# Bucketed attention and a maxout FFN: heads 4 to 7 of the first batch prepared as one set of four

## The chip, the cores and the metric

The kernel runs on one core of one Trainium2 chip. The metric is the device time of one execution in microseconds (us); lower is better. A core has five engines that run side by side, each through its own queue in order: TensorE (PE, with its weight loads PEld), VectorE (DVE), ScalarE (ACT), GpSimd (POOL) and SyncE (SP), which here only issues DMAs. POOL and ACT issue DMAs too.

## The reference: what is computed

Shapes: `q`, `k`, `v` are (4 batches, 8 heads, 768 tokens, 64), `proj` is (64, 6), the three input weights are (512, 768) and the output weight is (768, 512).

```python
def _attn_ref(q, k, v, proj):
    scale = 1.0 / np.sqrt(D)
    q_bits = (np.einsum('bhsd,dk->bhsk', q, proj) > 0)
    k_bits = (np.einsum('bhsd,dk->bhsk', k, proj) > 0)
    powers = 2 ** np.arange(n_bits)
    q_bucket = np.sum(q_bits * powers, axis=-1)
    k_bucket = np.sum(k_bits * powers, axis=-1)
    mask = q_bucket[:, :, :, None] == k_bucket[:, :, None, :]
    scores = scale * np.matmul(q, k.transpose(0, 1, 3, 2))
    scores = np.where(mask, scores, -1000000000.0)
    scores = scores - np.max(scores, axis=-1, keepdims=True)
    attn = np.exp(scores)
    attn = attn / (np.sum(attn, axis=-1, keepdims=True) + 1e-09)
    return np.matmul(attn, v)

def _moe_ref(x, w1, w2, w3, w_out):
    h = np.maximum(np.maximum(x @ w1, x @ w2), x @ w3)
    return h @ w_out
```

Each query attends only to the keys whose six hash bits equal its own. The attention's output, heads side by side, is the FFN's input.

## The kernel before

**How the mask enters.** For every head there is a tile S of 64 + 6 (later batches 64 + 8) rows by 768 tokens in bf16: the 64 scaled values of a token in a column, and under them its hash bits as +0.5 or -0.5. One matmul of a key tile's S with a query tile's S gives score plus a bonus for equal bits; the exponential's bias takes the bonus off again, so that tokens with a differing bit fall to nothing. What this study is about is how S is made.

**Units.** `units` cuts the attention into 192 units, 48 for each batch. A unit is one head, one chunk of queries (256 wide in batch 0, 384 later) and some key blocks: `scores(u)` (lines 277 to 301) puts 2 or 3 matmuls of S (L293) into one of two score buffers, and ACT takes the exponential of the buffer (L301). In batch 0 units 0 to 23 are heads 0 to 3 and units 24 to 47 heads 4 to 7, in the order head 4, 5, 6, 7 of chunk 0 first. So the S of head 4 is read first by unit 24.

**The order of work** is written out by hand. The last loop goes over u: at u it issues `scores(u + 1)`, then whatever `when(u, ...)` has put there, then FFN pieces by a credit, then the attention sums (L345) and values (L367) that `todo` has for u. Each engine executes its share in just that order. Sums and values of heads 0 to 3 stand at u = 20 to 30. A `hash_at` entry at u runs `quad_hash` at the end of u and puts the sending of its bits at u + 1. Later `when` entries for the same u stand behind earlier ones.

**Heads pair by pair (batch 0).** `load_pair` brings two heads of q and k into a tile `nat`, tokens in the partitions. `pair_group` turns three 128 x 128 blocks on PE against an identity (L120) and lets DVE copy the result from PSUM into `t32` (L129; for pair 1 in part ACT, L127). `pair_place` scales and narrows it to bf16 on POOL straight into S (L134). The bits of pairs 0 and 1 are computed head by head (`head_rest`, L167 on PE, L172 on DVE straight into S); pairs 2 and 3, heads 4 to 7, have `pair_hash`: four matmuls for a pair (L147), one DVE comparison into a tile `bits` (L150), and four DMAs from SP into S (L156). In `pair_hash` the transposed data are in fp32, as in all hashing.

**Heads in sets of four (batches 1 to 3).** A set is four heads of one side, q or k: set (1, g) is k, set (0, g) is q. `load_quad` brings each head with a DMA of its own into 32 partitions of `nat`. `turn` is one DVE transpose of 32 x 32 blocks (L198); a set needs four, u = 0, 1 for the half of the features and half = 0, 1. `narrow` scales a half of the features to bf16 on POOL (L203). The heads now lie under each other in partitions, so `place` moves each of the four with a DMA from SP into its S (L208). `quad_hash` computes all bits of q and k of four heads with eight matmuls (L217) and one comparison (L220); four more SP DMAs send them into S (L228).

**Queues that matter here.** SP carries, in this order: the first loads, the sends of bits of pairs 2 and 3, the loads of set 3 (u = 23 and 27), places and bits of set 2, and so on. POOL carries L134 and L203 and also issues the DMAs for V, the FFN weights and most `nat` loads: those of (1, 2) at u = 1 and (0, 2) at u = 13, V at u = 17, weights at u = 3, 12, 21, 31. A DMA issue waits until the one issued eight places earlier on the same kind of queue has landed.

Of the kernel before, what the change touches and what calls it, by code (L numbers as in the profile page):

```python
# [11 lines left out]
BF16 = mybir.dt.bfloat16  # L12
AluOp = mybir.AluOpType
# [4 lines left out]
def kernel(  # L18
# [12 lines left out]
    nc = tc.nc  # L31
    B, H, S, D = q.shape
    NBITS = proj.shape[1]
    P = 128
    NM = S // P
    HALF = S // 2
    MH = NM // 2
# [3 lines left out]
    Q = 32  # L41
    CC = P // Q
# [19 lines left out]
    b_pool = ctx.enter_context(tc.tile_pool(name="bpool", bufs=2))  # L62
# [13 lines left out]
    pj2 = konst.tile([P, Q], FP32, name="pj2")  # L76
# [11 lines left out]
    def bank():  # L88
        i = free_banks.pop(0)
        return i, bank_tiles[i]  # L90

    def give(i):
        free_banks.append(i)


    nat, t32, t16, s_of, where, v_at = {}, {}, {}, {}, {}, {}

    def start_set(name, heads):
        nat[name] = nat_pool.tile([P, 4 * NM * D], FP32, tag="nat", name="nat")
        for x, key in enumerate(heads):  # L100
            where[key] = (name, x)
# [7 lines left out]
    def load_pair(pi, eng, sides=(1, 0), h0=0, h1=2):  # L109
        if pi not in nat:  # L110
            start_set(pi, [(0, 2 * pi), (0, 2 * pi + 1), (1, 2 * pi), (1, 2 * pi + 1)])
        n = nat[pi].rearrange("p (s h w) -> p s h w", s=2, h=2)
        for side in sides:
            src = (q, k)[side][0, 2 * pi + h0 : 2 * pi + h1].rearrange("h (p c) d -> p h (c d)", p=P)
            eng.dma_start(n[:, side, h0:h1, :], src)
# [23 lines left out]
        pair_keep(pi, side, hd, mp, eng)  # L139
        give(i)  # L140

    def pair_hash(pi):
        i, bp = bank()
        for side in (1, 0):
            for hd in range(2):
                g = 2 * side + hd
                nc.tensor.matmul(bp[Q * g : Q * (g + 1), 0:HALF], pj2[:, :],  # L147
                                 t32[pi][:, side, hd * HALF : (hd + 1) * HALF], start=True, stop=True)
        bits = b_pool.tile([P, HALF], BF16, tag="bits", name="bits")
        nc.vector.tensor_scalar(out=bits[:], in0=bp[:, 0:HALF], scalar1=0.0, scalar2=0.5,  # L150
                                op0=AluOp.is_gt, op1=AluOp.subtract)
        give(i)
        for hd in range(2):
            for side in (1, 0):
                g = 2 * side + hd
                nc.sync.dma_start(s_of[pi][D : D + NBITS, g, :].rearrange("b (c n) -> b c n", c=2),  # L156
                                  bits[Q * g : Q * g + 2 * NBITS, :])


    def first_place(side, hd, par, mp):  # L160
        nc.scalar.mul(s_tile(0)[0:D, 2 * side + hd, par * HALF : (par + 1) * HALF],
                      mp[par * D : (par + 1) * D, 0:HALF], RS)
# [22 lines left out]
    def load_quad(side, g, xs, eng):  # L185
        if (side, g) not in nat:
            start_set((side, g), [(side, 4 * g + x) for x in range(4)])
        for x in xs:
            b, h = divmod(4 * g + x, H)
            src = (q, k)[side][b, h].rearrange("(cc t m) d -> t cc (m d)", cc=CC, t=Q)  # L190
            dst = nat[side, g][x * Q : (x + 1) * Q, :].rearrange("t (cc w) -> t cc w", cc=CC)
            eng.dma_start(dst, src)  # L192

    def turn(name, u, half):
        if name not in t32:
            t32[name] = t32_pool.tile([P, 2, S], FP32, tag="T32", name="T32")
        i_ = nat[name].rearrange("p (cc m u d) -> p u m cc d", cc=CC, u=2, d=Q)[:, u, half * MH : (half + 1) * MH]
        nc.vector.transpose(t32[name][:, u, half * HALF : (half + 1) * HALF], i_)  # L198

    def narrow(name, u):  # L200
# [244 lines left out]
    def when(u, f, *args):  # L445
        at.setdefault(u, []).append(lambda: f(*args))

    with tc.manual_schedule():
# [5 lines left out]
        load_pair(0, nc.sync, (1,), 1, 2)  # L454
        load_pair(0, nc.scalar, (0,), 1, 2)
        load_pair(1, nc.sync)
        load_pair(2, nc.sync)
        load_pair(3, nc.sync)
        nc.gpsimd.memset(pj[:], 0.0)
        nc.vector.memset(pj2[:], 0.0)  # L460
        nc.vector.memset(ones[:], 1.0)
# [44 lines left out]
            for par in range(2):  # L506
                pair_place(0, side, par, 1, 2)

        for pi, us in ((1, ((0, 1, 0), (0, 0, 0), (3, 1, 1), (4, 0, 1))), (2, ((6, 1, 0), (7, 1, 1), (8, 0, 0), (9, 0, 1))),
                       (3, ((13, 1, 0), (14, 1, 1), (15, 0, 0), (16, 0, 1)))):  # L510
            for u, side, hd in us:
                when(u, pair_group, pi, side, hd, nc.scalar if pi == 1 and hd == 1 else None)
                if pi == 1:
                    for par in range(2):
                        when(u, pair_place, pi, side, par, hd, hd + 1)
                elif hd == 1:
                    for par in range(2):
                        when(u, pair_place, pi, side, par)
        when(2, head_rest, 0, 1)
        when(2, t32.pop, 0)  # L520
        when(5, head_rest, 1, 0)
        when(10, pair_hash, 2)
        when(11, t32.pop, 2)
        when(11, head_rest, 1, 1)
        when(12, t32.pop, 1)
        when(17, pair_hash, 3)
        when(18, t32.pop, 3)
        when(1, load_quad, 1, 2, range(4), nc.gpsimd)
        when(17, load_v, 1)
        for n, u in ((0, 3), (1, 12), (2, 21), (3, 31)):  # L530
# [1 line left out]
        when(13, load_quad, 0, 2, range(4), nc.gpsimd)  # L532
        for u, side, g in ((23, 1, 3), (27, 0, 3)):
            when(u, load_quad, side, g, range(4), nc.sync)
        hash_at = {}
        for g in range(2, NQUAD):
            b2, i2 = divmod(g, 2)
            need = UPB * b2 + 12 * i2
            for n, side in enumerate((1, 0)):
                name = (side, g)  # L540
                if g > 3:
                    for x in range(4):
                        when(need - 36 + 4 * n + x, load_quad, side, g, (x,), nc.gpsimd)
                t0 = need - {2: 26, 3: 23}.get(g, 21) + 4 * n
                for n2 in range(4):
                    when(t0 + n2, turn, name, n2 // 2, n2 % 2)
                for u2 in range(2):
                    when(t0 + 2 + 2 * u2, narrow, name, u2)
                when(t0 + 6, place, name, range(4))
            hash_at[{2: 33, 3: 47}.get(g, need - 11)] = g  # L550
            when({2: 36, 3: 46}.get(g, need - 22), load_v, g)
# [4 lines left out]
        for c, i in sorted(done_at, key=lambda e: done_at[e]):  # L556
            d = done_at[c, i] + (LAG if c < 3 else 2)
            sums, values = burst(c, i)
            pieces = [lambda f=sums: f(0, NM), lambda f=values: f(0, 0, NM), lambda f=values: f(1, 0, NM)]
            for n, f in enumerate(pieces):  # L560
                u = {(0, 0): (20, 21, 22), (1, 0): (24, 25, 26), (2, 0): (28, 29, 30)}.get((c, i), (d, d, d))[n]
# [64 lines left out]
```

## Time and profile before

| | |
|---|---|
| time, median of 3 runs | 277.81 us (276.68 to 278.61) |
| the profiled execution's own time | 277.43 us |
| its span, first to last instruction | 275.6 us |
| mean granted TensorE clock | 0.992 |
| S of heads 4 to 7, pair by pair: PE turns L120, of 48 in all | 24 |
| one copy L129 on DVE | 0.49 us |
| one place L134, 64 x 768, on POOL | 0.83 us |
| one transpose L198 on DVE | 0.57 us, four end to end about 0.5 each |
| one narrow L203 on POOL, 128 x 768 | 0.82 us |
| one DMA issue L192 on POOL | 0.55 us |

The page gives first the busy time of each engine, then the span in 40 slices, the DMA queues, the chain of work that ended last, and the costliest groups of instructions. A timeline row reads: start in us from the span's start, duration, engine, line, operation, tiles, number of instructions merged, and in brackets how long the engine was idle before it and what ended that. SPq and POOLq are issues of DMAs by these engines' sequencers. PE's records are modelled at their ends and overlap a little. The trace also has the moments at which a DMA's completion signals arrive; where a landing time is given, it is the last of these for that DMA.

### The profile page before, as it was taken

Reading aid. Unit: us, or ns where it says so; the run is one execution under the profiler, and the core shown is the slowest. Engines: PE = TensorE matmul, PEld = TensorE weight load, DVE = VectorE, ACT = ScalarE, POOL = GpSimd, SP = SyncE. Lnnn points to the kernel's source line nnn. Section 1 sums busy time; section 2 is a strip of 40 time slices with the busy share of each in tenths; the row PEclk is TensorE's granted clock in tenths of the full one; section 3 lists DMA queues with packets and bytes.
Section 4 is the critical chain, followed back from the end, with each engine's and each line's share of the span. In section 5 each row is a group of like instructions: output and inputs, shape, how many; then the busy total and the mean of one; then the engine's idle time right before and its main releaser. Section 6 shows DMA issues by size and latency. Waiting matters only on the chain.

```text
span 275.6 us, 6502 instructions
## 1 busy us (share of the span) xinstructions
PE 263.2 (95%) x2538; PEld 158.6 (58%) x2538; DVE 196.0 (71%) x486; ACT 179.1 (65%) x260; POOL 68.0 (25%) x108
## 2 busy tenths in 40 slices
PE   7899999999999979999999999999999999999992
PEld 3555667865666645565555555555555555555651
DVE  3686787965886996996684898797657674865440
ACT  2888876648767860966859586683868769571321
POOL 3699550374100350285000062140000000000000
PEclk9999999999999997999999999999999999999999
DMA  7979999979921157169912036622020003001203
GB/s 226 287 158 165 221 245 227 209 125 231 246 49 40 38 145 115 53 183 251 168 40 76 2 81 148 160 57 63 33 95 0 1 4 114 2 0 40 76 2 114
DMA packets 20398, 30.97 MB, mean 112 GB/s; under 512 B 2608, under 2 KB 14736, under 8 KB 20368
## 3 DMA queue, kind: packets, MB, share of 16 engines
q0 software_dynamic: 8384, 14.16, 26.9%
q1 hardware_dynamic: 11552, 15.88, 19.2%
q10 hardware_dynamic: 432, 0.52, 0.6%
q8 instruction: 20, 0.33, 0.5%
q14 instruction: 10, 0.08, 0.1%
HBM read 25.17 MB, written 6.29 MB: 114 GB/s over the span
## 4 chain that ended last, share of the span: by engine, by line
PE 86%; DVE 7%; ACT 2%; issue 2%; DMA 1%; DVEq 0%; ACTq 0%
PE ms L396 31%; PE sc L293 22%; PE ms L367 11%; PE ms L433 11%; PE ms L345 4%; PE ms L217 3%; ACT AT L301 2%; DVE ad L324 2%; PE ms L472 1%; DVE ht L405 1%; PE ms L120 1%; PE ms L147 1%; PE ms L167 1%; DVE S L172 1%; DMA out_dram<-osb 1%
## 5 line engine op out<-in xcount | busy, mean ns | idle before, releaser
L301 ACT ACTIVATE AT<-sc 128x768 f16<-128x768 f32 x192 | 152.7, 816 | 66.4 <-PE sc L293 58.6
L396 PE MATMUL ms<-xT,w_sb 128*128 128x384 f16 (+1 forms) x648 | 115.0, 308 | 0.7 <-DVE ht L405 0.7
L293 PE MATMUL sc<-S 72*128 72x384 bf16 (+1 forms) x432 | 93.5, 308 | 2.6 <-ACT AT L301 1.9
L396 PEld LDWEIGHTS <-w_sb 128*128 128x128 f16 x648 | 62.6, 97 | 36.9 <-issue 1.5
L405 DVE TENSOR_TENSOR ht<-ht,ms 128x384 f16<-128x384 f16 (+1 forms) x108 | 54.3, 503 | 37.3 <-PE ms L396 35.4
L293 PEld LDWEIGHTS <-S 72*128 72x128 bf16 (+1 forms) x432 | 39.5, 98 | 34.0 <-issue 14.1
L203 POOL TENSOR_SCALAR T<-T 128x768 bf16<-128x768 f32 x24 | 21.8, 907 | 101.2 <-DVE T L198 80.4
L367 PE MATMUL ms<-AT,vo 128*32 128x385 f16 (+3 forms) x864 | 37.7, 318 | 0.0
L433 PE MATMUL ms<-wout_sb,ht 128*128 128x512 f16 x138 | 35.4, 378 | 0.0
L367 PEld LDWEIGHTS <-vo 128*32 128x32 f16 x864 | 25.1, 99 | 9.3 <-issue 1.3
L324 DVE TENSOR_TENSOR ad<-AT,AT 128x768 f16<-128x768 f16 x48 | 27.4, 572 | 2.8 <-ACT AT L301 2.8
L324 DVE TENSOR_TENSOR ad<-ad,AT 128x768 f16<-128x768 f16 x48 | 26.5, 551 | 2.5 <-ACT AT L301 1.2
L198 DVE STREAM_TRANSPOSE T<-nat 128x384 f32<-128x384 f32 x48 | 26.6, 561 | 0.0
L401 ACT CAST ht<-ms 128x384 f16<-128x384 f32 x36 | 17.2, 477 | 8.8 <-PE ms L396 8.7
L374 DVE SCALAR_TENSOR_TENSOR xT<-ms,sv,rb 128x384 f16<-128x384 f32 (+1 forms) x36 | 19.9, 568 | 2.6 <-PE ms L367 1.3
L433 PEld LDWEIGHTS <-ht 128*128 128x128 f16 x138 | 13.3, 97 | 13.3 <-DVE ht L405 0.8
L437 ACT COPY osb<-ms 128x512 f32<-128x512 f32 x23 | 13.4, 582 | 10.7 <-PE ms L433 9.6
L352 DVE STREAM_TRANSPOSE ys<-ms 128x384 f32<-128x384 f32 (+1 forms) x18 | 9.7, 536 | 8.0 <-PE ms L345 7.8
L134 POOL TENSOR_SCALAR S<-T 64x384 bf16<-64x384 f32 (+1 forms) x21 | 13.2, 627 | 3.8 <-ACT T L127 1.6
L192 POOL DMA_DIRECT2D nat<-in_k_dram x20 | 11.1, 563 | 3.6 <-DMA nat<-in_k_dram 2.2
L192 POOL DMA_DIRECT2D nat<-in_q_dram x20 | 11.1, 566 | 2.7 <-DMA vo<-in_v_dram 1.8
L345 PEld LDWEIGHTS <-ones 128*32 128x32 f16 x240 | 5.4, 95 | 8.8 <-issue 8.7
(48 smaller groups left out, 121.9 us busy)
## 6 DMA issues: line engine op xcount, KB each, us to landing
out_dram<-osb SPq DMA_DIRECT2D x23, 256.0 KB
S<-T SPq DMA_DIRECT2D x48, 96.0 KB
nat<-in_k_dram POOLq DMA_DIRECT2D x20, 192.0 KB, 7.5
nat<-in_q_dram POOLq DMA_DIRECT2D x20, 192.0 KB, 7.1
vo<-in_v_dram POOLq DMA_DIRECT2D x8, 384.0 KB, 8.2
w_sb<-in_moe_w_dram POOLq DMA_DIRECT2D x3, 768.0 KB, 7.2
nat<-in_k_dram SPq DMA_DIRECT2D x6, 192.0 KB
nat<-in_k_dram SPq DMA_DIRECT2D x3, 384.0 KB
```

The costliest lines, as they stand in the source:

```text
L192: eng.dma_start(dst, src)
L198: nc.vector.transpose(t32[name][:, u, half * HALF : (half + 1) * HALF], i_)
L203: nc.gpsimd.tensor_scalar(out=t16[name][:, u, :], in0=t32[name][:, u, :], scalar1=RS, scalar2=1.0, op0=AluOp.mult, op1=AluOp.mult)
L293: nc.tensor.matmul(views[j], s_of[kn][0 : D + bits, kx, m * P : (m + 1) * P], s_of[qn][0 : D + bits, qx, q0 : q0 + w], start=True, stop=True)
L301: nc.scalar.activation(t[:, :, 0:w], whole, ActFn.Exp, bias=-SCALE * 0.25 * bits, scale=SCALE)
L324: nc.vector.tensor_tensor(out=sum_of[c, h][:], in0=t[0], in1=t[n], op=AluOp.add)
L367: nc.tensor.matmul(av[Q * x : Q * (x + 1), 0:n], v_at[2 * b + i][:, x, cb * D + side : (cb + 1) * D : 2], weights_of(c, 4 * i + x, m)[:, 0 ...
L374: nc.vector.scalar_tensor_tensor(out=xt_of(c)[:, 2 * i + side, 0:w], in0=av[:, 0:w], scalar=sv_of[b, i, side][:], in1=rb[0][:, 0:w], op0=A ...
L396: nc.tensor.matmul(ps[:, 0:w], w_sb[wi][:, jc, fb * P : (fb + 1) * P], xt[:, jc, 0:w], start=(jc == 0), stop=(jc == NJC - 1))
L401: nc.scalar.copy(hts[fb][:, 0:w], ps[:, 0:w])
L405: nc.vector.tensor_tensor(out=hts[fb][:, 0:w], in0=hts[fb][:, 0:w], in1=ps[:, 0:w], op=AluOp.max)
L433: nc.tensor.matmul(ps[:, 0:DM], hts[fb][:, tb * P : (tb + 1) * P], wout_sb[:, fb, :], start=(fb == 0), stop=(fb == NFB - 1))
```

## The change

Heads 4 to 7 of batch 0 become sets (1, 1) for k and (0, 1) for q. The loads of pairs 2 and 3 (four DMAs of two heads each) become eight DMAs of one head each, k first. The 24 PE turns, eight DVE copies, eight POOL places and two `pair_hash` of these pairs go. In their place come four DVE turns and two POOL narrows for k at u = 6 to 9 and the same for q at u = 10, 12, 13, 14, four place DMAs behind each (u = 9 and u = 14), one `quad_hash` at u = 16, and its four sends at u = 17. `turn` takes every second token block for g = 1, since batch 0 keeps its tokens in the pairs' order (`block_of`). The new `when` entries stand in the program behind those for loads and weights. On POOL the order from u = 7 on is thus: narrow and narrow of k, one weight load (u = 12), first narrow of q (u = 12), the four loads of set (0, 2) (u = 13), second narrow of q (u = 14), then V and weights. On SP it is: eight loads, four places of k, four places of q, four sends of bits, then the loads of set 3.

```diff
-    def pair_hash(pi):
-        i, bp = bank()
-        for side in (1, 0):
-            for hd in range(2):
-                g = 2 * side + hd
-                nc.tensor.matmul(bp[Q * g : Q * (g + 1), 0:HALF], pj2[:, :],
-                                 t32[pi][:, side, hd * HALF : (hd + 1) * HALF], start=True, stop=True)
...
-                nc.sync.dma_start(s_of[pi][D : D + NBITS, g, :].rearrange("b (c n) -> b c n", c=2),
-                                  bits[Q * g : Q * g + 2 * NBITS, :])
...
     def turn(name, u, half):
...
-        i_ = nat[name].rearrange("p (cc m u d) -> p u m cc d", cc=CC, u=2, d=Q)[:, u, half * MH : (half + 1) * MH]
+        ms = slice(half, NM, 2) if name[1] == 1 else slice(half * MH, (half + 1) * MH)
+        i_ = nat[name].rearrange("p (cc m u d) -> p u m cc d", cc=CC, u=2, d=Q)[:, u, ms]
         nc.vector.transpose(t32[name][:, u, half * HALF : (half + 1) * HALF], i_)
...
         load_pair(1, nc.sync)
-        load_pair(2, nc.sync)
-        load_pair(3, nc.sync)
+        for side in (1, 0):
+            load_quad(side, 1, range(4), nc.sync)
...
-        for pi, us in ((1, ((0, 1, 0), (0, 0, 0), (3, 1, 1), (4, 0, 1))), (2, ((6, 1, 0), (7, 1, 1), (8, 0, 0), (9, 0, 1))),
-                       (3, ((13, 1, 0), (14, 1, 1), (15, 0, 0), (16, 0, 1)))):
+        for pi, us in ((1, ((0, 1, 0), (0, 0, 0), (3, 1, 1), (4, 0, 1))),):
...
-                elif hd == 1:
-                    for par in range(2):
-                        when(u, pair_place, pi, side, par)
...
-        when(10, pair_hash, 2)
-        when(11, t32.pop, 2)
         when(11, head_rest, 1, 1)
         when(12, t32.pop, 1)
-        when(17, pair_hash, 3)
-        when(18, t32.pop, 3)
         when(1, load_quad, 1, 2, range(4), nc.gpsimd)
...
-        hash_at = {}
+        for side, us in ((1, (6, 7, 8, 9)), (0, (10, 12, 13, 14))):
+            for n, u in enumerate(us):
+                when(u, turn, (side, 1), n // 2, n % 2)
+                if n % 2:
+                    when(u, narrow, (side, 1), n // 2)
+            when(us[3], place, (side, 1), range(4))
+        hash_at = {16: 1}
```

More of the change, by code (lines that the diff above doesn't have):

```diff
@@ L140, in pair_group @@
         give(i)
-    def pair_hash(pi):
-        i, bp = bank()
-        for side in (1, 0):
-            for hd in range(2):
-                g = 2 * side + hd
-                nc.tensor.matmul(bp[Q * g : Q * (g + 1), 0:HALF], pj2[:, :],
-                                 t32[pi][:, side, hd * HALF : (hd + 1) * HALF], start=True, stop=True)
[L149 to L155, printed above, removed]
-                nc.sync.dma_start(s_of[pi][D : D + NBITS, g, :].rearrange("b (c n) -> b c n", c=2),
-                                  bits[Q * g : Q * g + 2 * NBITS, :])
     def first_place(side, hd, par, mp):
```

## The prediction

> **What bounds the kernel now.** I read the page's busy shares and its chain first, for the engine that sets the end, and then the timelines of ACT, PE, POOL and SP around the changed units, for what that stretch waits on.
>
> ```profile
> PE 263.2 (95%) x2538; PEld 158.6 (58%) x2538; DVE 196.0 (71%) x486; ACT 179.1 (65%) x260; POOL 68.0 (25%) x108
> ...
> PE 86%; DVE 7%; ACT 2%; issue 2%; DMA 1%; DVEq 0%; ACTq 0%
> ```
>
> TensorE sets the end over the whole span. But the page's share is an average, and the changed work lies in units 6 to 17. ACT's timeline there:
>
> ```profile
> 14.87 4.37 ACT L301 ACTIVATE AT<-sc 128x768 f16<-128x768 f32 x6
> 20.61 0.81 ACT L301 ACTIVATE AT<-sc 128x768 f16<-128x768 f32 x1 [1.37 <-PE sc L293]
> 21.80 4.40 ACT L301 ACTIVATE AT<-sc 128x768 f16<-128x768 f32 x6 [0.39 <-PE sc L293]
> 27.00 2.21 ACT L301 ACTIVATE AT<-sc 128x768 f16<-128x768 f32 x3 [0.80 <-PE sc L293]
> ```
>
> These are units 6 to 11, 12, 13 to 18, and 19 to 21. Inside a run one exponential follows the other every 0.72 us (4.37 less the last one's 0.81, over 5): here ACT is the bound, and PE has room. ACT waits only at the three hashes: 1.37 behind the first `pair_hash`, 0.39 behind `head_rest`, 0.80 behind the second. PE's timeline shows where that ends:
>
> ```profile
> 27.86 0.49 PE L293 MATMUL sc<-S 70*128 70x256 bf16 x3 [0.57 <-ACT AT L301]
> 28.28 0.84 PE L345 MATMUL ms<-AT,ones 128*32 128x256 f16 x24
> 29.05 0.50 PE L293 MATMUL sc<-S 70*128 70x256 bf16 x3
> 29.49 0.85 PE L367 MATMUL ms<-AT,vo 128*32 128x257 f16 x24
> 30.27 0.50 PE L293 MATMUL sc<-S 70*128 70x256 bf16 x3
> 30.70 0.85 PE L367 MATMUL ms<-AT,vo 128*32 128x257 f16 x24
> ```
>
> Unit 21's scores (27.86) are the last that wait for ACT; from then on PE is full to the end but for some 3 us. So whatever moves unit 21 moves the end, and any later wait of PE is paid whole. The next L293 row starts at 31.49: unit 24, the first that reads the S of head 4.
>
> **The change, part by part.**
>
> *PE turns, copies, places that go.* The 24 turns are about 2.7 us of PE (groups of three, 0.34 from row to row), but at units 6 to 11 ACT ran without a gap over them: worth nothing. DVE loses eight copies of 0.49 and gains eight transposes of about 0.5: even. POOL loses eight places of 0.83 and gains four narrows of 0.82.
>
> *Hashes.* The two `pair_hash` and their waits of 1.37 and 0.80 go; one `quad_hash` comes (42.70 to 44.13 in set 2: 1.43 of PE). I step the engines with the rows' durations. ACT ends unit 10 at 18.5, so unit 12's scores, `head_rest` and unit 13's scores stand 1.55 earlier than now (18.5 for 20.07), and ACT starts unit 13 at 20.25 and unit 17 at 23.1. DVE: bits of `head_rest(1, 0)` until 17.3, four turns of k until 19.3, one of q until 19.8, then the bits of `head_rest(1, 1)`, 2.26 for four, until 22.1, and the other three turns of q at 22.7, 23.2 and 23.65. The hash stands behind unit 17's scores (22.5). Its second half needs the last turn, so it starts at 23.7 and PE goes on 0.75 later, at 24.45; ACT starts unit 18 at 25.0 (0.54 behind its scores, as now) against 25.4 now, unit 19 at 25.7 against 27.0, and unit 21's scores come at 26.55 against 27.86. **Gain: 1.3.** Unit 24 could start at 31.49 - 1.3 = 30.2.
>
> *The way of S to unit 24.* This is what is late next. POOL does the narrow of q's first half at 22.75 to 23.6 (second turn at 22.7). Behind it stand the four loads of set (0, 2), now at
>
> ```profile
> 23.22 2.23 POOL L192 DMA_DIRECT2D nat<-in_q_dram  x4
> ```
>
> so the second narrow of q runs from about 26.0 to 26.85. SP must hold the four places of q until then, and the sends of bits, though the bits are ready at 25.1, stand behind them in SP's queue. Set 3 shows the same eight issues with nothing to hold them:
>
> ```profile
> 56.65 2.49 SPq L208 DMA_DIRECT2D S<-T  x4
> 59.33 2.94 SPq L228 DMA_DIRECT2D S<-bits  x4
> ```
>
> The third send, q's first half of the tokens, starts 4.2 us behind the first place. Unit 24 waits for it: 26.9 + 4.2 = 31.1. Already the issue is later than 30.2. How long it takes to land is the open price. By the completion signals the sends of the second `pair_hash`, at 27.15 to 29.45 and alone on their queue, landed 5.1 to 6.2 us later, while POOL's weights and loads filled the DMA engines (share over 1 in that stretch). From below: the fastest send of the trace took 2.6 (21.77 to 24.4). From above: in set 3 the third send landed 13.9 behind the first place (56.65 to 70.5), with POOL's loads beside it. Set 2, 44.02 to 54.6, gives 10.6. As landing times that is 33.7, 36.3 (31.1 + 5.2), 37.5 and 40.8. I take 37.0, between the two that are nearest in place and in order. **PE waits from 30.2 to 37.0: 6.8.** Nothing covers it: PE's queue is in order, and sums of the next chunk, values and scores all stand behind unit 24. The places of k are free (narrowed by 20.65, sent by 23), as are the first loads: the eighth issues at about 8.4, and what SP loads now lands by 14.4, before the first turn at 17.3.
>
> *The clock.* What does PE pay after so long a wait? The trace has one such place, in windows of PE busy, PEld, DVE, ACT, POOL, granted clock, DMA share, GB/s:
>
> ```profile
> 102.00:104.00 2.00, 0.38 (x7) 0.13 (x10) 1.90 (x6) 0.21 (x1) 1.28 (x2) 1.00 0.10 14
> 104.00:106.00 2.00, 2.00 (x28) 1.27 (x31) 1.39 (x5) 0.00 (x0) 0.00 (x0) 0.51 0.92 100
> 106.00:108.00 2.00, 2.00 (x36) 1.31 (x29) 1.04 (x2) 0.00 (x0) 0.00 (x0) 0.64 1.19 238
> ```
>
> After two mostly idle microseconds the clock is halved from 104.0 to 107.5, and the chain gives 48 L367 matmuls 3.37 there against 1.97 elsewhere. **1.4 more.** [...]
>
> **Sum.** -1.3 + 6.8 + 1.4 = **+6.9**. The profiled execution took 277.4 (its span of 275.6 and 1.8 around it), 0.4 under the median of the three runs; I predict **284.3 us**.
>
> **The rivals.**
>
> *S lands fast.* SP alone feeds its queue then, and 24 KB is little. At the fastest latency, 2.6, the bits land at 33.7: a wait of 3.5, less 1.3, and too short for a halved clock: +2.2, 279.6. For it: the first sends of the trace. Against it: those had only one weight load beside them; here two more, V and four loads are queued. [...] Chance 0.13.
>
> *S comes in time, and the kernel is faster.* Place: SP's queue. If the second narrow of q and SP's eight issues ran some 7 us earlier than I step them (bits landed by 30.2, the point from which it decides), only the gain of 1.3 would remain: 276.1. For it: set 2's S had 1.5 us to spare at unit 48 (landed by 54.8, read at 56.32). Against it: the order of POOL and SP is fixed, and the transposes stand behind 2.26 us of bits on DVE. Chance 0.05.
>
> *The queue is shared as in set 3.* Landing at 40.8: a wait of 10.6, one or two halved windows: -1.3 + 10.6 + 1.4 to 2.8, +10.7 to +12.1, 288 to 289.5. For it: set 3 has the same eight DMAs in the same order beside POOL loads of the same kind. Against it: there eight such loads were issued right beside the places, here four, already under way. Chance 0.12.
>
> **Chances and range.** My own case has 0.70, with landings from 35.6 to 39.4: 282.9 to 286.7. The range reaches from the fast landing, 279.6, to the foot of the third rival, 288.0. About 1% (2.8 us) is what a measurement can tell from no change: faster by more needs twice the gain I find, 0.02; within it lie the fast landing and the case in time, 0.16; slower 0.82.
>
> **What would show it.** A wait of PE before the second-half scores (unit 24, about 30 to 37), ended by DMAs into S, and ACT idle for about 7 us with it; the ACT gap behind the first `pair_hash` gone, and a gap of about 1.2 at unit 18; unit 21's scores near 26.5; a clock of 0.5 for a few us after the wait; POOL's second narrow of q right behind four L192 issues; SP's places of q from about 27. Wrong would be: scores of unit 24 following at once (then S was in time); PE's row at 26.5 not earlier than now (then DVE's turns hold the hash longer). A step of the clock somewhere else, as at 104, is worth 1.4 by itself.

## The result, and the profile after

| | before | after |
|---|---|---|
| median of four runs each | 277.88 us (276.68 to 278.61) | 290.98 us (287.76 to 291.76) |
| profiled execution, and its span | 277.43, 275.6 | 291.76, 290.0 |
| mean granted TensorE clock | 0.992 | 0.946 |

The ratio is 1.045 (95% interval 1.036 to 1.054): 13.1 us slower. 284.3 had been forecast, with a range up to 288.0. The direction holds, the size is twice what was forecast. Line numbers of the kernel after are lower by 17 or 18: scores L276, exponential L284, sums L328, values L350, `turn` L181, `narrow` L186, `place` L191, `quad_hash` L200, its sends L211.

The page of the kernel after, busy time by engine and two rows of the 40 slices (7.25 us each):

```profile
PE 271.3 (94%) x2514; PEld 158.8 (55%) x2514; DVE 195.8 (68%) x485; ACT 179.3 (62%) x260; POOL 64.9 (22%) x104
...
PE   7989939999999998799999999999999999999993
...
PEclk9985575999999999799999999999999999999999
```

PE is 8.1 us busier with 24 instructions fewer: the same matmuls take longer. The row PEclk says why. Slices 3 to 7 have a clock of 0.5 to 0.8, and before had 0.9 or more in all of them; the 7 further right is the old place at 104, now at 118. The slice with a 3 in PE's row is the forecast wait. So two things are seen, and only one of them had been expected where it starts.

ACT's timeline of the kernel after, units 6 to 12 in the first row:

```profile
15.34 5.15 ACT L284 ACTIVATE AT<-sc 128x768 f16<-128x768 f32 x7
21.78 1.51 ACT L284 ACTIVATE AT<-sc 128x768 f16<-128x768 f32 x2 [1.29 <-PE sc L276]
23.47 1.51 ACT L284 ACTIVATE AT<-sc 128x768 f16<-128x768 f32 x2 [0.18 <-PE sc L276]
25.17 0.81 ACT L284 ACTIVATE AT<-sc 128x768 f16<-128x768 f32 x1 [0.18 <-PE sc L276]
28.64 1.51 ACT L284 ACTIVATE AT<-sc 128x768 f16<-128x768 f32 x2 [2.66 <-PE sc L276]
...
41.98 1.51 ACT L284 ACTIVATE AT<-sc 128x768 f16<-128x768 f32 x2 [5.81 <-PE sc L276]
```

The wait of 1.37 behind the first `pair_hash` is gone as forecast: unit 12's exponential runs on without a gap. But the next waits are longer than those of before (1.29 for 0.39, 2.66 for 0.80). PE's timeline shows what ACT waits for:

```profile
18.35 0.49 PE L276 MATMUL sc<-S 70*128 70x256 bf16 x3 [0.21 <-ACT AT L284]
...
25.06 2.79 PE L200 MATMUL ms<-T,pj 128*32 128x384 f32 x16
27.78 1.46 PE L276 MATMUL sc<-S 70*128 70x256 bf16 x6
...
33.08 1.48 PE L350 MATMUL ms<-AT,vo 128*32 128x257 f16 x24
34.50 0.82 PE L276 MATMUL sc<-S 70*128 70x256 bf16 x3
35.25 1.48 PE L350 MATMUL ms<-AT,vo 128*32 128x257 f16 x24
41.08 1.44 PE L276 MATMUL sc<-S 70*128 70x256 bf16 x6 [4.35 <-issue]
```

A burst of 24 values takes 1.48 where it took 0.85, a score of three matmuls 0.82 for 0.50, the `quad_hash` 2.79 where the same sixteen matmuls take 1.50 later on. Then, at 41.08, comes unit 24 after 4.35 us of nothing. The windows of the kernel after, cut where the clock changes (us, PE busy, PEld, DVE, ACT, POOL, granted clock, DMA share, GB/s):

```profile
12.84:16.26 3.42, 3.02 (x27) 1.60 (x26) 2.96 (x6) 3.34 (x7) 3.26 (x7) 1.00 1.03 231
16.26:19.68 3.42, 2.48 (x19) 1.40 (x23) 3.33 (x7) 3.42 (x6) 3.03 (x7) 1.00 1.00 191
19.68:23.09 3.41, 3.15 (x17) 1.21 (x11) 2.57 (x6) 2.12 (x4) 2.19 (x3) 0.50 0.96 187
...
33.33:36.74 3.41, 3.40 (x51) 1.62 (x43) 1.66 (x5) 1.48 (x2) 0.00 (x0) 0.50 1.22 226
36.74:40.16 3.42, 0.00 (x0) 0.00 (x0) 1.58 (x4) 0.00 (x0) 0.82 (x1) 1.00 1.08 230
40.16:43.57 3.41, 2.49 (x30) 1.49 (x30) 0.00 (x0) 1.51 (x2) 0.00 (x0) 0.50 1.09 238
43.57:46.98 3.41, 3.41 (x46) 1.50 (x42) 2.58 (x7) 0.87 (x2) 0.83 (x1) 0.50 0.95 204
46.98:50.40 3.42, 3.42 (x50) 1.96 (x46) 1.55 (x4) 2.08 (x3) 0.83 (x1) 0.50 0.45 111
```

In before, PE is busy through the same units; its window there, in the same columns:

```profile
16.00:19.40 3.40, 3.40 (x28) 2.30 (x26) 3.19 (x7) 3.24 (x5) 3.08 (x6) 1.00 0.88 174
```

In after, the clock is halved from 19.68, 17 us ahead of the wait, just behind the window in which PE had little but scores to do (19 matmuls, one score every 0.70 us, where ACT is the bound). It stays halved for five windows, is full in the window in which PE does nothing, and is halved for three more windows, to 50.40, after the wait.

POOL's and SP's timelines of the kernel after, where S of heads 4 to 7 is made:

```profile
24.00 0.82 POOL L186 TENSOR_SCALAR T<-T 128x768 bf16<-128x768 f32 x1 [1.99 <-DVE T L181]
24.88 2.25 POOL L174 DMA_DIRECT2D nat<-in_q_dram  x4
27.19 0.83 POOL L186 TENSOR_SCALAR T<-T 128x768 bf16<-128x768 f32 x1
```

```profile
21.21 9.30 SPq L191 DMA_DIRECT2D S<-T  x8
30.61 3.03 SPq L211 DMA_DIRECT2D S<-bits  x4
```

This order is the forecast one, an issue of four loads between the two narrows of q and the bits behind all places, some 1.2 us later than stepped. The third send of bits is issued at 32.27, and by its completion signals it lands at 41.0; PE goes on at 41.08.

Against before, the 14.4 us between the two spans are then: unit 24 could start at 36.7 instead of 31.5, 5.2 later (0.5 of it a later start of the whole kernel); the wait, 4.35; the halved clock behind it, 4.15 more between 41 and 50.4; 0.7 in the rest. The first two are one sum: unit 24 starts 9.6 later, and what it starts on is the landing of S at 41.0, so a PE that came sooner would only wait longer (the first experiment shows it).

### The profile page after: what moved, and what is told of

It reads as the page before. It is cut to its first block, busy times and chain, and to the rows that moved or that the text cites. A ratio compares the mean times of both kernels' runs of the same rounds, so it can differ in the third digit from the quotient of the medians.

```text
span 290.0 us, 6458 instructions
## 1 busy us (share of the span) xinstructions
PE 271.3 (94%) x2514; PEld 158.8 (55%) x2514; DVE 195.8 (68%) x485; ACT 179.3 (62%) x260; POOL 64.9 (22%) x104
## 4 chain that ended last, share of the span: by engine, by line
PE 78%; DVE 8%; ACT 4%; DMA 3%; issue 3%; POOL 1%; SPq 1%; DVEq 0%; ACTq 0%
PE ms L379 28%; PE sc L276 19%; PE ms L350 11%; PE ms L416 10%; PE ms L328 4%; ACT AT L284 3%; PE ms L200 3%; DMA S<-bits 3%; DVE ad L307 2%; DVE S L154 2%; PE ms L455 1%; DVE ht L388 1%; PE ms L149 1%; DVE T L181 1%; SPq L191 1%
## 5 line engine op out<-in xcount | busy, mean ns | idle before, releaser
L284 ACT ACTIVATE AT<-sc 128x768 f16<-128x768 f32 x192 | 152.9, 815 | 80.1 <-PE sc L276 72.2
L276 PE MATMUL sc<-S 72*128 72x384 bf16 (+1 forms) x432 | 98.7, 325 | 8.9 <-issue 4.7
L379 PEld LDWEIGHTS <-w_sb 128*128 128x128 f16 x648 | 62.7, 97 | 36.8 <-issue 1.5
L276 PEld LDWEIGHTS <-S 72*128 72x128 bf16 (+1 forms) x432 | 41.2, 102 | 45.3 <-issue 21.5
L186 POOL TENSOR_SCALAR T<-T 128x768 bf16<-128x768 f32 x28 | 25.1, 897 | 117.4 <-DVE T L181 89.0
L350 PE MATMUL ms<-AT,vo 128*32 128x385 f16 (+3 forms) x864 | 40.2, 334 | 0.0
L350 PEld LDWEIGHTS <-vo 128*32 128x32 f16 x864 | 25.6, 103 | 11.0 <-issue 1.6
L181 DVE STREAM_TRANSPOSE T<-nat 128x384 f32<-128x384 f32 x56 | 30.6, 560 | 0.0
L307 DVE TENSOR_TENSOR ad<-ad,AT 128x768 f16<-128x768 f16 x48 | 26.5, 552 | 2.5 <-ACT AT L284 1.2
L416 PEld LDWEIGHTS <-ht 128*128 128x128 f16 x138 | 13.4, 97 | 13.1 <-DVE ht L388 0.6
L200 PE MATMUL ms<-T,pj 128*32 128x384 f32 x112 | 12.2, 543 | 0.0
L328 PEld LDWEIGHTS <-ones 128*32 128x32 f16 x240 | 5.9, 106 | 9.8 <-issue 9.0
```

What stands on the lines that cost most here:

```text
L186: nc.gpsimd.tensor_scalar(out=t16[name][:, u, :], in0=t32[name][:, u, :], scalar1=RS, scalar2=1.0, op0=AluOp.mult, op1=AluOp.mult)
L200: nc.tensor.matmul(bp[Q * r : Q * (r + 1), 0:HALF], pj[:, u, :], ts[side][:, u, j * HALF : (j + 1) * HALF], start=(u == 0), stop=(u == 1))
L276: nc.tensor.matmul(views[j], s_of[kn][0 : D + bits, kx, m * P : (m + 1) * P], s_of[qn][0 : D + bits, qx, q0 : q0 + w], start=True, stop=True)
L284: nc.scalar.activation(t[:, :, 0:w], whole, ActFn.Exp, bias=-SCALE * 0.25 * bits, scale=SCALE)
L307: nc.vector.tensor_tensor(out=sum_of[c, h][:], in0=t[0], in1=t[n], op=AluOp.add)
L350: nc.tensor.matmul(av[Q * x : Q * (x + 1), 0:n], v_at[2 * b + i][:, x, cb * D + side : (cb + 1) * D : 2], weights_of(c, 4 * i + x, m)[:, 0 ...
```

## The experiments

Theory 1, formed from these views: the whole loss is (a) a clock that falls because the 24 turns of PE are gone from units 6 to 17, and (b) the way of S to unit 24, with the halved clock behind that wait. Its rivals are that the clock falls for another reason than the missing turns, or that the wait alone explains the loss.

**PE kept busy where the turns were.** Three turns of the identity into a PSUM bank of their own, the kind of work that the change removed, at each of units 6 to 19.

```diff
+    def keep_busy():
+        i, mp = bank()
+        for n in range(MH):
+            nc.tensor.transpose(mp[:, n * P : (n + 1) * P], iden[:], iden[:])
+        give(i)
...
+        for u in range(6, 20):
+            when(u, keep_busy)
```

> The changed kernel plus a filler on TensorE: at each of units 6 to 19 three 128x128 fp32 turns of the identity into a spare PSUM bank that nobody reads (42 turns, about 0.36 us a unit, in PE's room beside the exponential's 0.72). Theory 1 (the missing turns let the clock fall at 19.7): granted clock 1.0 up to the wait, unit 24's scores ready at about 31 instead of 36.7; but S still lands at about 40 to 41, since POOL's and SP's order and the load on the DMA engines stay, so the wait grows from 4.4 to 9 or 10 us, the clock falls in it, and the time is 289 to 292, about that of the changed kernel. Theory 2 (the clock's fall at 19.7 has another cause): clock 0.5 from about 20 as in the changed kernel, unit 24 ready at 36 to 38, 290 to 293.

Measured 290.43 us, ratio 1.043 (1.037 to 1.049). PE's timeline of this run:

```profile
26.50 1.50 PE L206 MATMUL ms<-T,pj 128*32 128x384 f32 x16
...
32.87 0.85 PE L356 MATMUL ms<-AT,vo 128*32 128x257 f16 x24
42.24 1.44 PE L282 MATMUL sc<-S 70*128 70x256 bf16 x6 [8.52 <-DMA nat<-in_k_dram]
43.61 1.47 PE L334 MATMUL ms<-AT,ones 128*32 128x256 f16 x24
```

The `quad_hash` is back at 1.50 and the values at 0.85: the clock is 1.0 from 15.2 to 35.68, through the stretch in which it had been halved. So it is the missing work that let the clock fall here. The time hardly changes, 0.5 us and within the noise, since PE arrives 3.0 us earlier (33.72 for 36.73) and waits for S all the longer, 8.52: the third send of bits, issued at 33.66, lands at 42.15, and PE goes on at 42.24. (The releaser named on the row is a load that lands later; by the signals it is the bits.) Behind the wait the clock is again halved until 49.33. So in the changed kernel the clock lost ahead of unit 24 is hidden behind the wait, and what sets the time is the landing of S and the clock after it. The profiled execution also has a halved window ahead of the identity turns, 11.79 to 15.20, behind a wait of 0.58 for the q of pair 1; more on that at the end of this section.

**No wait for S.** The changed kernel, in which the scores of heads 4 to 7 of batch 0 read the S of heads 0 to 3; the S of heads 4 to 7 is still made.

```diff
-        (qn, qx), (kn, kx) = where[0, b * H + h], where[1, b * H + h]
+        hs = b * H + h - (4 if b == 0 and h >= 4 else 0)
+        (qn, qx), (kn, kx) = where[0, hs], where[1, hs]
```

> The changed kernel, but the scores of heads 4 to 7 of batch 0 read the S of heads 0 to 3 (their q, k and bits, so the values of these heads are others); turns, narrows, places and bits of heads 4 to 7 are still done and read by nobody. So the wait for S is gone and all work stays. Theory 1: the clock falls at about 19.7 all the same and is back at about 37; no wait before unit 24, no second fall; 5.2 us (unit 24 at 36.7 for 31.5) over before, 283 to 284. Theory 2 (all the loss hangs on the wait): 276.5 to 278.

Measured 281.56 us, ratio 1.011 (1.005 to 1.017), between the two forecasts. The wait and what it brings behind it are thus worth 9.4 of the 13.1 us. The windows of this run around the fall of the clock, columns as above:

```profile
17.73:21.14 3.41, 2.67 (x23) 1.26 (x22) 3.15 (x7) 3.08 (x5) 3.09 (x6) 1.00 0.96 173
21.14:24.55 3.41, 2.41 (x22) 1.19 (x20) 3.35 (x7) 3.36 (x5) 1.98 (x3) 1.00 1.01 193
24.55:27.96 3.41, 3.15 (x20) 1.12 (x16) 0.56 (x2) 1.32 (x3) 3.22 (x7) 0.50 1.00 175
```

The clock falls here with no wait of PE longer than 0.57 us in the two windows before, behind a window with 2.41 of 3.41 us busy, and stays halved until 34.79: three windows, not five. One of the four runs, 279.01 us at a mean clock of 0.993, loses little.

**Both together.**

> Both: filler on TensorE at units 6 to 19, and heads 4 to 7 of batch 0 read the S of heads 0 to 3 (other values; their own S is made and not read). This leaves only the gain that I had put at 1.3 us. Theory 1: clock 1.0 through units 6 to 30, no wait, 276 to 278 (the filler may cost a few tenths at the hash). If the filler does not hold the clock up: like the run without filler, 283 to 284.

Measured 279.37 us, ratio 1.003 (0.999 to 1.006, ten runs). With the wait gone, the clock ahead of unit 24 is worth another 2.2 us in the medians; the intervals of the two runs overlap, so that this is a rough figure. What remains against before, 1.5 us in the medians (the interval includes no change), misses the 276 to 278 expected, and it is not the gain of 1.3 that I had forecast for the changed kernel without its wait. The profiled execution, at 281.93 us the longest of the ten, shows two losses that Theory 1 leaves out: a wait of 0.68 for the q of pair 1 with a halved window behind it (12.96 to 16.37), and a stop of PE of 1.01 us up to 39.27, in the middle of the values, for which the profile names no releaser.

**The kernel before, without its 24 turns.** The other direction: only the turns of pairs 2 and 3 are left out (DVE still copies the banks, so heads 4 to 7 hold no right data).

```diff
-        pair_turn(pi, side, hd, mp)
+        if pi < 2:
+            pair_turn(pi, side, hd, mp)
```

> The kernel before, with the 24 PE turns of pairs 2 and 3 left out (DVE copies what stands in the bank, so S and bits of heads 4 to 7 hold no meaningful values); all else as before, the two pair hashes too. Theory 1: with PE half idle in units 6 to 9 the clock falls in a window near 16 to 23 and PE becomes the bound there: unit 24 later by 2 to 6 us, 280 to 284. Theory 2: PE had room, so the turns cost nothing and save nothing: 277 to 278, clock 0.99.

Four runs: 283.32, 283.15, 283.32 and 279.0 us, median 283.23. With 2.7 us of PE's work taken away, the kernel is no faster in any of them, and 5.4 us slower in three. (The ratio on record, 1.0105 with an interval of 1.0004 to 1.0207, takes in only two of the runs, 283.15 and 279.0; in the run of 279.0 the mean clock was 0.999, in the other three 0.962 to 0.964.) Its windows, columns as above:

```profile
14.58:17.99 3.41, 2.38 (x18) 1.27 (x17) 3.28 (x7) 3.41 (x6) 3.17 (x6) 1.00 0.95 233
17.99:21.41 3.42, 3.42 (x16) 0.96 (x19) 1.45 (x3) 1.09 (x3) 3.04 (x5) 0.50 0.99 159
21.41:24.82 3.41, 2.41 (x21) 1.20 (x14) 2.58 (x5) 2.91 (x5) 3.41 (x6) 1.00 0.73 109
24.82:28.23 3.41, 3.41 (x16) 1.12 (x16) 1.83 (x5) 2.24 (x3) 2.78 (x4) 0.50 1.08 218
```

Twice a window with 2.4 us of PE, scores and little else, is followed by a halved one. The kernel before has a mean clock of 0.990 to 0.999 in every one of its runs here; the profiled one, with the window at 104 alone, has 0.992, so none of them had room for windows like these. So the turns, which cost nothing on the path, had been holding the clock; one run escaped, and on what that hangs no run shows.

**S sooner, clock kept.** Then the way of S, with the identity turns in place. POOL's four loads of set (0, 2) go two units later; of the places of q only head 4's stay ahead of the bits.

```diff
-        when(13, load_quad, 0, 2, range(4), nc.gpsimd)
+        when(15, load_quad, 0, 2, range(4), nc.gpsimd)
...
-            when(us[3], place, (side, 1), range(4))
+            if side == 1:
+                when(us[3], place, (side, 1), range(4))
+            else:
+                when(us[3], place, (side, 1), (0,))
+                when(18, place, (side, 1), (1, 2, 3))
```

> The changed kernel with the filler on TensorE at units 6 to 19 and another order on two queues: POOL narrows both halves of q before it issues the four loads of set (0, 2) (moved from u = 13 to 15), and SP sends the place of head 4's q first, then the four sends of bits, then the other three places of q. Theory A (the wait is queue order plus a landing of 5 to 9 us among POOL's loads): head 4's q is sent about 2 us earlier, q's first bits about 4 earlier than in the run with filler alone; they land at 34 to 38 instead of 42, the wait falls from 8.5 to 2 to 6 us, the clock still falls after it: 282 to 288. Theory B (the order of SP does not matter, the DMA engines finish these small transfers only when POOL's backlog is through): landing at 40 to 42 as before, 289 to 291.

Measured 284.55 us, ratio 1.022 (1.018 to 1.027). SP's and then PE's timeline:

```profile
27.30 3.05 SPq L217 DMA_DIRECT2D S<-bits  x4
```

```profile
36.40 0.81 PE L282 MATMUL sc<-S 70*128 70x256 bf16 x6 [4.03 <-DMA S<-bits]
```

The bits leave 4.7 us earlier than with the identity turns alone, and the wait is shorter by 4.5: 8.52 to 4.03. (POOL's order and SP's were changed together, so their shares are not told apart.) The releaser is now named on the row. Each of the four still takes 7.2 or 7.3 us from its issue until it has landed (34.5 to 36.8).

**Other DMAs out of the way.** In addition V goes from u = 17 to 25 and the second and third weights from u = 12 and 21 to u = 26 and 27.

> The run before (filler, new order of POOL and SP) with POOL's other loads put off: V of heads 4 to 7 from u = 17 to 25, the second and third weight from u = 12 and 21 to 26 and 27, so that from about 25 to 34 only the loads of set (0, 2) stand beside the places and bits. Theory A: these land 2.5 to 4 us after their issue, by 29 to 32, the wait before unit 24 is 0 to 2 us; but the weights come some 8 us later, and the FFN may wait for the third: 278 to 283. Theory B (the landing time of places and bits does not hang on POOL's loads): landing as in the run before, and the late weights on top: 285 or more.

Measured 281.14 us, ratio 1.011 (1.007 to 1.015). PE's row of unit 24:

```profile
33.39 0.81 PE L282 MATMUL sc<-S 70*128 70x256 bf16 x6 [1.87 <-DMA S<-bits]
```

The bits, sent from 26.45, land by 33.5. The same four DMAs, without V and the two weights, take 4.7 to 6.3 us instead of 7.2 or 7.3, though not the 2.5 to 4 expected: how long these 24 KB take hangs here on what else is queued. A wait of 1.87 is still followed by a halved window (35.23 to 38.64).

**Work put into the wait.** All sums and values of heads 0 to 3 moved ahead of unit 24, on the queue order of "S sooner, clock kept" (V and weights back in their places), with identity turns at units 24 to 32 also.

```diff
-                u = {(0, 0): (20, 21, 22), (1, 0): (24, 25, 26), (2, 0): (28, 29, 30)}.get((c, i), (d, d, d))[n]
+                u = {(0, 0): (20, 21, 21), (1, 0): (21, 22, 22), (2, 0): (22, 22, 22)}.get((c, i), (d, d, d))[n]
```

> The run with the new order of POOL and SP, and sums and values of all three query chunks of heads 0 to 3 put at u = 20 to 22, before unit 24's scores, instead of u = 20 to 30; filler on TensorE also at units 24 to 32, which now have little else. PE then has about 4.9 us of work where it waited (sums 0.77 and two values 0.85 for each of two chunks). Theory A: unit 24 starts at about 36 with a wait of 0 to 2 us and a full clock, ACT runs units 24 to 33 at 0.72 each, the FFN begins at 45 to 47 as in the kernel before (44.5): 278 to 281. If the pulled-up work only moves the wait (ACT then binds units 24 to 35 and PE idles): 281 to 284.

Measured 284.50 us, ratio 1.021 (1.016 to 1.026), no better than the order alone and longer than either forecast. PE's timeline:

```profile
33.94 0.38 PE L334 MATMUL ms<-AT,ones 128*32 128x256 f16 x6
36.94 1.25 PE L334 MATMUL ms<-AT,ones 128*32 128x256 f16 x18 [2.62 <-issue]
```

PE now idles 2.62 us in the middle of the moved sums, the clock is halved from 36.45 to 39.86, and unit 24 starts at 40.3; from there ACT is the bound, since the scores are late and PE has nothing left to put beside them. The matmul at which PE goes on waits for nothing in the program, and the profile names no releaser. The stop stands behind PE's 705th instruction in the trace (weight loads counted), just as the stop of 1.01 in the run with both edits does, and a stop of 1.26 in the run without the wait stands 256 instructions further; in all three a load of 16 KB on the queue that the page calls "instruction" ends 1.4 to 1.7 us before PE goes on. That PE waits for its own program there is an estimate from these times that no run tests, and whether filling the wait would have paid without this stop stays open.

**The quiet stretch of the kernel before.** If 1.5 us of turns hold the clock, they should also mend the one halved window of before, at 104, where PE waits for DVE (rows of the prediction). Fourteen identity turns go into a free part of the sums' bank there.

```diff
+            if (c, i) == (4, 0):
+                for n in range(14):
+                    nc.tensor.transpose(sm[:, HALF : HALF + P], iden[:], iden[:])
```

> The kernel before, nothing moved, but 14 turns of the identity (1.5 us of PE) into columns 384 to 511 of the bank of the sums of the first query chunk's heads 0 to 3 of batch 1's second half (at about 102, where PE waits for VectorE's additions); nobody reads them. If a mostly idle window is what halves the clock at 104.0: it stays at 1.0 there, the 48 values behind take 1.95 instead of 3.37, and 1 to 1.5 us go: 276 to 277. If the fall has another cause or 1.5 us of turns is not enough: 277.5 to 279, clock 0.5 at 104 as now.

Measured 276.59 us, ratio 0.9959 (0.9938 to 0.9980, twelve runs): 0.4% faster than before, and clear of the noise. The values in before, then PE's timeline and one window of this run:

```profile
104.22 3.86 PE L367 MATMUL ms<-AT,vo 128*32 128x384 f16 x48
```

```profile
102.96 1.75 PE L345 MATMUL ms<-iden 128*128 128x128 f32 x14 [0.43 <-DVE ht L406]
104.64 0.60 PE L348 MATMUL ms<-ad,ones 128*32 128x384 f16 x8
104.97 2.22 PE L370 MATMUL ms<-AT,vo 128*32 128x384 f16 x48
```

```profile
104.00:107.50 3.50, 3.50 (x71) 3.16 (x73) 3.05 (x8) 0.00 (x0) 0.13 (x1) 1.00 0.84 102
```

The 48 values take 2.22 for 3.86, and the clock is 1.00 where it was 0.51 to 0.64. Here work that computes nothing pays for itself by the clock, 1.4 us in the medians.

**Everything put back.** The changed kernel with all that these runs had found: identity turns beside the scores of units 7 to 20, this time in free columns of the scores' own buffer, so that they wait for no bank; q turned at u = 9 to 12 and hashed at 13, ahead of the second `head_rest`; head 4's place first, then the bits (now first halves of k and q, then second halves, in every set), then the other places; the loads of (0, 2) at u = 15, weights at u = 25 and 27; and the fourteen turns of the last run.

```diff
+        if 7 <= u <= 20:
+            for n in range(MH):
+                nc.tensor.transpose(sc[:, 1, HALF : HALF + P], iden[:], iden[:])
...
-        when(11, head_rest, 1, 1)
+        when(14, head_rest, 1, 1)
...
-        for side, us in ((1, (6, 7, 8, 9)), (0, (10, 12, 13, 14))):
+        for side, us in ((1, (6, 7, 8, 9)), (0, (9, 10, 11, 12))):
...
-        hash_at = {16: 1}
+        hash_at = {13: 1}
```

> The changed kernel with everything put back that the earlier runs showed to be missing: three identity turns beside each of units 7 to 20's scores, in free columns of their own tile (so that they wait for no bank of their own); the turns of q at units 9 to 12 and their hash at 13, ahead of the second head_rest; of the places of q only head 4's ahead of the bits, the three others behind; POOL's loads of set (0, 2) two units later, the second and third weights at units 25 and 27; and the 14 identity turns of the run with before's quiet stretch filled (276.6). Theory 1 (the lost time is the clock and the way of S and nothing else, and the set form by itself is worth nothing): 276 to 278, no wait of more than 1 us at unit 24, clock 1.0 from about 7 to the end. Theory 1 with the gain that I had forecast for the set form (1.3): 275 to 275.6. Rival (the first set's S cannot be had by unit 24 in this form whatever the order, its loads and DMAs being too late): a wait of 2 us or more before unit 24's scores and 279 to 282.

Measured 277.42 us, ratio 0.9996 (0.9968 to 1.0025, twelve runs). PE's timeline:

```profile
24.03 1.50 PE L200 MATMUL ms<-T,pj 128*32 128x384 f32 x16
...
34.06 0.85 PE L356 MATMUL ms<-AT,vo 128*32 128x257 f16 x24
34.85 0.83 PE L276 MATMUL sc<-S 70*128 70x256 bf16 x6
```

Unit 24 (34.85) follows with no wait, at full clock. It comes 3.4 us later than in before here, and the first half of q's bits has landed by 34.3, so the margin is small; no trace shows an execution in which PE arrives sooner. Against the changed kernel 13.6 us are won back, of which some 1.3 belong to the turns at 104, so that clock and wait account for about 12 of the 13.1. With the identity turns that it needs, the form is worth nothing: the kernel equals before although the turns at 104, which made before 0.4% faster, are in it. The forecast of 1.3 for it, 275 to 275.6, is not met. Part of the reason stands in PE's timeline of this run, a little earlier:

```profile
10.05 0.49 PE L120 MATMUL ms<-iden,nat 128*128 128x128 f32 x3
11.29 0.55 PE L120 MATMUL ms<-iden,nat 128*128 128x128 f32 x3 [0.75 <-DMA nat<-in_q_dram]
```

The q of pair 1 lands at 11.25; in before it had landed at 8.4 and in after at 10.3. It is issued just ahead of the eight loads of the sets (in after at 2.61, the first of them at 3.12), and they are under way when it lands. In this execution the wait of 0.75 was followed by a halved window (12.07 to 15.49), 2.2 us together at unit 4; ten of the twelve runs have a mean clock of 0.997 or more and so no such window. The same wait and window stand in the two profiled executions above. From unit 4 to unit 11 another 0.9 goes, as ACT waits 0.17 to 0.19 for the identity turns in its buffer before every second exponential, and from unit 11 to unit 24 the kernel loses 0.2 against before, where I had it gaining 1.3.

## Why the prediction was right or wrong, point by point

**Which terms made the number.** +6.9 was forecast; between the two profiled spans it is 14.4 (13.1 in the medians). Unit 24 was to start at 37.0 and started at 41.08: 4.1 more, of which 1.2 is a later send and 2.8 a longer time to land. The halved clock behind the wait was to cost 1.4 and cost 4.15: 2.75 more. The last 0.7 had no term. These two terms put the time above the range. Another step failed earlier in the kernel, but there it hides behind the wait.

**PE's turns are "worth nothing": wrong, though not what made the number.** The turns were rightly found to be off the path, since ACT bounds units 6 to 11. What failed is the conclusion that removing them is free. They filled PE's windows: with them 28 matmuls and 3.40 of 3.40 us in before (16.0 to 19.4), without them 19 and 2.48. The clock fell behind that window. Taking them out of before did the same without anything else of the change (283.2 in three of four runs), and putting idle turns into after undid it; but in after that is worth only 0.5 us, within the noise, because S is later still, and some 2 us once nothing waits for S. I had a section on the clock, but asked only what follows a wait; a stretch in which another engine is the bound and PE works half of the time was not looked at. In the window ahead of the fall at 19.68 PE stands still for only 0.20 to 0.40 us at a time, once before each of the five scores; the clock fell there without a wait like the 1.45 us that end at 103.96 in before, just ahead of its fall at 104.0.

**The gain of 1.3: not found.** Its first half was right: ACT starts unit 12 1.4 us earlier than before, measured from a common start (forecast 1.55). The second half was mis-sized: the `quad_hash` was to cost 0.75 on PE and leave a gain at unit 18. In after it runs at half clock and unit 18 is 3.25 late. At full clock (the run with the identity turns, up to its wait), unit 12 again comes 1.4 earlier, counted from unit 6; then unit 13 gives back 0.4, a bank that DVE holds costs the identity turns 0.85 at unit 16, and unit 18 loses 1.35 against unit 17, of which unit 19 returns 0.9: 0.3 is lost at unit 21. With the identity turns in the scores' buffer it is again none.

**The way of S: right in its mechanism, late by 4 us.** Narrow behind four loads, places behind the narrow, bits behind the places, PE waiting at unit 24 with all queued behind it: each is in the rows. The third send was forecast at 31.1 and came at 32.27; the landing was forecast at 37.0, with bounds from 33.7 to 40.8, and came at 41.0. The term that was mis-sized is the time to land, 5.9 us forecast and 8.7 measured: from the first place of q, 28.05, it took 12.9, and the row of set 3 had 13.9, set 2 10.6. I had set the former aside (0.12) for the eight loads beside it, but here, too, the DMA engines were full (a share of 1.07 to 1.22 in the windows from 26.5 to 43.6): the sets' first loads ran on to 18.5 instead of 14.4, and V, weights and loads followed. With the neighbours moved away the same sends took 4.7 at the least. The wait itself was 4.35 instead of 6.8, only because the clock had made PE late for it; with the clock held it is 8.52.

**The halved clock after the wait: 4.15 instead of 1.4.** The row at 104 showed one window of 3.4 us. Here it lasted three, 40.16 to 50.40, though PE had work from 41.08 on and is busy for the whole of the second one. With waits of 1.87 and 4.03 it lasted one window, with 8.52 four, the first of them without any work. Why three here and not one stays open.

**The rivals.** S did not land fast, nor in time. The first rival's sum has nothing for the clock, since it held a wait of 3.5 too short for a halved one; no run shows such a limit, and here a wait of 1.87 was followed by a halved window, as were waits of 0.58 to 0.75 for the q of pair 1. The queue shared as in set 3 is what happened to the landing (41.0 for 40.8), and the time it was given, 288 to 289.5, is 1.5 us short of the median, by the clock. I gave this rival 0.12 and let the range end at its foot, 288.0; that is why it ended too low. No case of mine had a loss ahead of unit 24 either, but holding the clock there still gave 290.43.

**What would show it.** Of the list, the vanished gap behind the first `pair_hash`, the wait with ACT idle, POOL's narrow behind four loads and the late places of q came as named. Unit 21's scores at 26.5 did not: they came at 30.2. The text had DVE in mind for that, and a step of the clock "somewhere else" as a side remark, at 1.4.

## What to carry to other kernels

Work of TensorE that hides behind another engine may be what keeps its clock up: before removing it, or moving it to another engine, count what is left for PE in each 3.41 us, the window of the clock in these traces, where it is not the bound, and price the stretch at half speed as a rival if it is only scores with gaps between (2.38 to 2.48 us busy here, and a clock of 0.50 behind). What that costs shows only where no longer wait lies behind it (0.5 us ahead of the wait for S, some 2 without that wait). A short run of idle turns in a stretch that PE must wait through anyway can pay for itself (0.4% here). And a tile that travels by DMA needs its landing time from a row with the same queues full, not from one with the same bytes (24 KB took 8.7 us in after, and 4.7 to 6.3 with V and two weights moved away).

## What the runs showed of the hardware that was not expected

- In the traces here the steps of the clock in an execution lie on one grid of 3.41 us: in after 36.74, 40.16, 50.40 and 118.66 are 5, 6, 9 and 29 windows behind 19.68. That the same gap may cost a window or nothing by where it falls is an estimate from this grid, and no run tests it; one of the four runs of before without its turns kept its clock (279.0 us, mean 0.999).
- How busy PE looks does not tell by itself whether the clock falls. It fell behind windows with 2.38, 2.41 and 2.48 us of modelled PE time made of scores, held behind 2.67 in the window ahead of one of these, and held in the run with the new order behind a window with only 1.89 (30.48 to 33.90), 51 matmuls packed together ahead of a gap. It also rose at 36.74 and 21.41, after windows of 3.4 us busy, and did not rise at 46.98 after another such. What makes the clock step is not settled by these runs.
- Turns of an identity in fp32 held the clock here: with three at each unit from 17.3 to 30.2 it was full from 15.2 to 35.68, and with fourteen it was full in the window at 104.
- In after the eight loads of 196 KB into 32 partitions each land 0.7 to 1.5 us apart and end at 18.5 us, the last two issued at 8.31 and 10.32, each right behind the landing (8.29, 10.31) of the load issued eight places earlier; the two-head loads of 393 KB into 128 partitions that they replaced follow one another by about 1.05 at first and end at 14.4. The same bytes take longer, and the load of pair 1's q, issued ahead of them, lands 1.9 to 2.9 us later.
